# A fused recurrence and mixture-of-experts kernel: the loads of two expert passes are issued later, behind copies of the experts' numbers

## The chip, the cores and the metric

The kernel runs on one core of a Trainium2 chip. A core has five engines that run their own instruction streams: TensorE (PE in the profile; its weight loads are PEld), VectorE (DVE), ScalarE (ACT), GpSimd (POOL) and SyncE (SP). Here SP does little but issue transfers. Transfers run on 16 DMA engines that all queues share. The metric is the device time of one execution in microseconds. Three runs before the change took 410.62, 410.77 and 410.91 us.

## The reference

Two blocks follow each other. The first is a recurrence over 768 steps for 4 batches and 8 heads of dimension 48: a state of 48 x 48 per head decays by a gate, takes in an outer product of key and value, and is read by the query. The second takes the 3072 rows of 384 numbers that come out, chooses one of 4 groups and one of 4 experts in it for every row, and applies that expert's two-layer network.

```python
f = 1.0 / (1.0 + np.exp(-f_logit))
for t in range(S):
    state = f[:, :, t, :, None] * state + np.einsum('bhd,bhe->bhde', k[:, :, t], v[:, :, t])
    y[:, :, t] = np.einsum('bhd,bhde->bhe', q[:, :, t], state)
...
x = attn_out.transpose(0, 2, 1, 3).reshape(B * S, H * D)        # 3072 x 384
g_idx = argmax(x @ w_group)                                     # 4 groups
e_idx = argmax(x @ w_expert[g_idx])                             # 4 experts in each
h = np.maximum(xg[mask_e] @ w1[g, e], 0.0)                      # 384 -> 1024
out[tok_idx] = (g_w * e_w)[:, None] * (h @ w2[g, e])            # 1024 -> 384
```

An expert has 1.57 MB of weights in each of its two layers (w1 and w2); there are 16 experts.

## The kernel before

**Two stages.** Up to about 140 us the recurrence runs in chunks of 128 steps, and each finished chunk is routed: the experts of its rows are chosen and counted, and the rows are written to a table in DRAM (`x_dram`). When the last chunk is routed, the experts have been ranked by their load. `rows_p` then holds, for every place in the ranking, the addresses of the rows of that expert; `who` (cast at L300 in `named`) holds the experts' numbers as integers on one partition.

**Early work.** Places 0 and 1 are fixed before the last chunks: their weights are loaded already during the recurrence (`load_next`, behind copies of their numbers in `who_late`), and `early()` takes 128 rows of each through both layers around 131 to 153 us.

**The passes.** Then come 16 passes, n = 0 to 15, one for each entry of `PLACES`: place 0 again (the rest of its rows), places 2 to 15, and place 1 last. The texts below call n = 1 the second pass and n = 2 the third. A pass has these parts:

- `pass_of(n)` calls `fetch` (L404): indirect gathers of the pass's rows from `x_dram` into a tile `xg`, issued by POOL. Six `xg` tiles exist.
- The rows are turned so that features lie on the partitions, into `xe`: by TensorE with copies behind it (`turn_in`, L440 and L441) for n = 0 and 1 and the last, by VectorE's transposes of 32 x 32 squares (`square_in`, L426) for the others.
- `up` (L450 on TensorE, L451 on ScalarE): the first layer, from `w1`.
- `down` (L486, or `down_rows` at L471 for passes of 128 rows): the second layer, from `w2`.
- The result is turned back (`square_out`, L433), scaled (L458) and scattered to `out` by POOL (L461).

The loop over n is written by hand so that `up` of pass n + 1 stands before `down` of pass n on TensorE. Before the loop, `turn_in(ws[0])`, two steps of `up` of n = 0, `turn_in(ws[1])`, and the rest of `up` of n = 0.

**The loads.** `load_weights` reads one number from `who` into a register of SP (`value`, L388, a TENSOR_LOAD) and issues the transfers of both layers (`load_layer`, L392). The buffers come from two pools: `wp` with two of each layer, which the two early experts hold at first, and `wq` with one of each layer, used by n = 1, 4, 7 and so on. A load waits until the buffer that it takes is no longer read. The engines TensorE, VectorE, ScalarE and SP run in the order in which the code is written (`manual_schedule`); POOL's order is the framework's. So SP issues: both layers of n = 1, both of n = 2, then inside the loop, after each `down(n)`, both layers of n + 3. A waiting load holds up everything behind it on SP.

Of the kernel before, what the change touches and what calls it, by code (L numbers as in the profile page):

```python
# [11 lines left out]
I32 = mybir.dt.int32  # L12
# [11 lines left out]
def kernel(  # L24
# [12 lines left out]
    nc = tc.nc  # L37
# [5 lines left out]
    GE = G * EG  # L43
# [25 lines left out]
    wp = ctx.enter_context(tc.tile_pool(name="wp", bufs=2))  # L69
# [7 lines left out]
    def const(shape, dtype, name):  # L77
        return cp.tile(shape, dtype, tag=name, name=name)

    def bank(shape, name):  # L80
        return ps.tile(shape, FP32, tag="bank", name=name)
# [189 lines left out]
    who = const([1, GE], I32, "who")  # L271
# [115 lines left out]
    def value(ap, top):  # L387
        return nc.values_load(ap, engines=(ET.SP,), min_val=0, max_val=top, skip_runtime_bounds_check_because="a table that the routing makes within these bounds")  # L388

    def load_layer(pool, e, layer):  # L390
        w = pool.tile([P, KO, F] if layer == 1 else [P, FO, DM], FP32, tag=f"w{layer}", name=f"w{layer}")
        nc.sync.dma_start(out=w, in_=(w1v if layer == 1 else w2v)[bass.ds(e, 1)].rearrange("o p k f -> (o p) k f"))  # L392
        return w

    def load_weights(pool, ap):
        e = value(ap, GE - 1)
        return load_layer(pool, e, 1), load_layer(pool, e, 2)
# [9 lines left out]
    def room(w, shape, name):  # L407

        full = w["pool"].tile([P, shape, P if w["pool"] is ep else WIDE], FP32, tag=name, name=name)
        w[name[:2].replace("xe", "xT") + "_full"] = full  # L410
        return full[:, :, 0:w["n"]]

    def squares(w, turn):


        for k_ in range(P // SQ):
            n = sum(j * P + k_ * SQ < w["n"] for j, m in w["blocks"])
            for g in range(P // SQ):
                turn(n, k_, slice(k_ * SQ, (k_ + 1) * SQ), g, slice(g * SQ, (g + 1) * SQ))

    def square_in(w):

        w["xT"] = room(w, KO, "xe")
        x = w["x"][:, :, 0:DM].rearrange("p j (o g c) -> p j g o c", o=KO, c=SQ)
        xT = w["xT_full"].rearrange("p o (j k c) -> p j k o c", j=2, c=SQ)
        squares(w, lambda n, k_, rk, g, rg: nc.vector.transpose(out=xT[rg, 0:n, k_], in_=x[rk, 0:n, g]))  # L426

    def square_out(w):

        w["rows"] = w["pool"].tile([P, 2, DM], FP32, tag="yr", name="yr")  # L430
        y = w["rows"].rearrange("p j (o g c) -> p j g o c", o=KO, c=SQ)
        yT = w["yT_full"].rearrange("p o (j k c) -> p j k o c", j=2, c=SQ)
        squares(w, lambda n, k_, rk, g, rg: nc.vector.transpose(out=y[rk, 0:n, g], in_=yT[rg, 0:n, k_]))  # L433

    def turn_in(w):
        w["xT"] = room(w, KO, "xe")
        for j, m in w["blocks"]:
            pt = bank([P, KO, P], "xg_ps")
            for ko in range(KO):
                nc.tensor.transpose(out=pt[:, ko, 0:m], in_=w["x"][0:m, j, ko * P:(ko + 1) * P], identity=ident[0:m, 0:m])  # L440
            (nc.scalar.copy if w["early"] else nc.vector.tensor_copy)(w["xT"][:, :, j * P:j * P + m], pt[:, :, 0:m])  # L441
# [34 lines left out]
    def down(w, w2):  # L476
        n = w["n"]
        if n == P:
            for _ in down_rows(w, w2):
                pass  # L480
            return
        w["yT"] = w["yT_full"][:, :, 0:n]
        for m in range(KO):
            yp = bank([P, n], "yo")
            for fo in range(FO):
                nc.tensor.matmul(yp, lhsT=w2[:, fo, m * P:(m + 1) * P], rhs=w["h"][:, fo, :], start=(fo == 0), stop=(fo == FO - 1))  # L486
            nc.scalar.copy(w["yT"][:, m, :], yp)  # L487

    def scaled(w, settle=False):
        if w["n"] > P:  # L490
            for j, m in w["blocks"]:
                with settled(settle and j):
                    put(w, j, m, w["rows"][:, j, :])
# [413 lines left out]
    wq = main.enter_context(tc.tile_pool(name="wq", bufs=1))  # L907
# [3 lines left out]
    PLACES = [0] + list(range(EARLY, GE)) + list(range(1, EARLY))  # L911

    def pass_of(n):
        p = PLACES[n]
        if p < EARLY:
            return fetch(mo, rows_p[:, p, 1:2], P)
        return fetch(mo, rows_p[:, p, :], WIDTHS[p - EARLY])

    fari = const([1, 1], I32, "fari")

    def weakest():

        worst = const([P, 1], FP32, "worst")
        nc.vector.tensor_reduce(out=worst, in_=decays.rearrange("p c a n -> p (c a n)"), axis=AX, op=OP.min)
        wt = bank([1, P], "wt")
        nc.tensor.transpose(out=wt, in_=worst, identity=ident)
        far = const([1, 2], FP32, "far")
        nc.vector.tensor_reduce(out=far[:, 0:1], in_=wt, axis=AX, op=OP.min)
        nc.vector.tensor_scalar(far[:, 1:2], far[:, 0:1], math.exp(-SAFE), None, OP.is_lt)
        nc.vector.tensor_copy(fari, far[:, 1:2])  # L930

    def flags():

        nc.vector.tensor_copy(both[:, 0:1], fari)
        nc.vector.tensor_scalar(rest, b_end, 0, None, OP.is_gt)
        nc.vector.tensor_tensor(both[:, 1:2], fari, rest, OP.max)
# [1 line left out]
    both = const([1, 2], I32, "both_i")  # L938
    rest = const([1, 1], I32, "rest")
    ws = {n: pass_of(n) for n in range(3)}  # L940
    ahead = {n: load_weights(wq if n % 3 == 1 else wp, who[0:1, PLACES[n]:PLACES[n] + 1]) for n in range(1, 2)}
    ahead[0] = weights[0]

    def const_out(i):
# [5 lines left out]
    def run_up(n):  # L950
        for _ in up(ws[n], ahead[n][0]):
            pass
# [6 lines left out]
    next(opening)  # L959
    next(opening)  # L960
    turn_in(ws[1])
    for _ in opening:
        pass
    for n in range(GE - 1):
        w = ws[n]
        if n + 3 < GE:
            ws[n + 3] = pass_of(n + 3)
        if n == 0:
            ahead[2] = load_weights(wp, who[0:1, PLACES[2]:PLACES[2] + 1])
        past, coming = ws.pop(n - 1, None), ws.get(n + 2)  # L970
        if past and past["n"] > P:
            square_out(past)
        if coming and coming["n"] > P:
            square_in(coming)
        if n + 2 < GE:
            run_up(n + 1)
        if past:

            scaled(past, n == GE - 3)
        if coming and coming["n"] == P:  # L980
            turn_in(coming)
        w["yT_full"] = outs[n % 2]
        down(w, ahead.pop(n)[1])
        if n + 3 < GE:
            ahead[n + 3] = load_weights(wq if n % 3 == 1 else wp, who[0:1, PLACES[n + 3]:PLACES[n + 3] + 1])
        if n == 2:
            with tc.tile_pool(name="tb", bufs=1) as tb:
                beyond(False, tb)
        if n == 3:
            weakest()  # L990
            flags()
# [133 lines left out]
```

## Time and profile before

| | |
|---|---|
| median of three runs | 410.77 us (410.62 to 410.91) |
| the profiled execution | 410.61 us, of it 408.8 us the span that the profile covers |
| granted TensorE clock, mean | 0.999 |
| TensorE busy | 401.3 us, 98% |
| VectorE busy | 264.9 us, 65% |
| ScalarE busy | 162.9 us, 40% |
| POOL busy | 86.0 us, 21% |
| weight loads on SP's queue | 34 of 1536 KB, 10.9 us median from issue to landing |
| gathers of rows (L404) | 30, 6.7 us median to landing |
| all transfers | 88.99 MB, 218 GB/s over the span |

Times in the profile are microseconds from the start of the span. A row of a group names the line, the engine, the operation, what is written and what is read; a waits row says which engine's line stood idle for whom. Busy times of a pipelined TensorE come with modelled ends.

### The profile page before, as it was taken

The page shows a single profiled execution, that of the slowest core. Times are in us where ns is not written, and L with a number is a line of the kernel's source. Part 1 is how long each engine was busy: PE and PEld are TensorE (multiplying, and loading weights), DVE is VectorE, ACT ScalarE, POOL GpSimd, SP SyncE. Part 2 cuts the span into 40 slices and gives each one's busy share as a digit, 9 for nine tenths or more (in the row PEclk, how much of TensorE's full clock was granted, in tenths as well). Part 3 has the DMA queues.
Part 4 walks back from the last instruction along what each step waited for, and adds up shares of the span by engine and source line. Part 5 has one row for each costly group of instructions (what it writes and reads, how often), then busy time and mean ns, then how long its engine had stood idle before and what let it go on. Part 6 is the DMA issues. An engine that isn't in the chain of part 4 may idle for free.

```text
span 408.8 us, 10274 instructions
## 1 busy us (share of the span) xinstructions
PE 401.3 (98%) x4143; PEld 369.6 (90%) x4143; DVE 264.9 (65%) x783; ACT 162.9 (40%) x365; POOL 86.0 (21%) x132
## 2 busy tenths in 40 slices
PE   8999999999999999999999999999999999999994
PEld 3888888888888969799999999999999999999992
DVE  6666887887998805601999749468576586585230
ACT  6777888888564202121312123122121222222130
POOL 5000010102040084011222123220411310120240
PEclk9999999999999999999999999999999999999999
DMA  9999988789969599993846739468487596485010
GB/s 188 204 216 211 197 176 175 149 164 270 276 214 375 198 319 331 349 326 80 311 138 246 249 135 356 138 257 296 130 327 224 175 354 227 148 314 164 28 50 22
DMA packets 132146, 88.99 MB, mean 218 GB/s; under 512 B 102582, under 2 KB 122748, under 8 KB 132090
## 3 DMA queue, kind: packets, MB, share of 16 engines
q1 hardware_dynamic: 125666, 75.50, 62.0%
q0 software_dynamic: 5792, 11.92, 9.7%
q10 hardware_dynamic: 632, 0.83, 0.6%
q8 instruction: 35, 0.57, 0.5%
q14 instruction: 21, 0.17, 0.1%
HBM read 78.71 MB, written 9.83 MB: 217 GB/s over the span
## 4 chain that ended last, share of the span: by engine, by line
PE 52%; issue 30%; DMA 8%; POOL 6%; DVE 2%; POOLq 1%; ACT 0%; SPq 0%; DVEq 0%
PE hp L450 12%; DMA out_dram<-yt,xg 7%; PE yo L486 7%; PE yo L471 4%; PE cs L616 4%; POOL out_dram L461 4%; PE x_ps L795 3%; PE tr_q L650 3%; PE tr_k L650 3%; PE y L746 3%; PE y L754 2%; PE ap L704 2%; PE ap L689 2%; POOL xg L404 2%; PE ds L722 2%
## 5 line engine op out<-in xcount | busy, mean ns | idle before, releaser
L450 PE MATMUL hp<-xe,w 128*128 128x128 f32 (+14 forms) x864 | 138.6, 320 | 0.0
L450 PEld LDWEIGHTS hp<-xe,w 128*128 128x128 f32 x864 | 135.8, 190 | 0.8
L433 DVE STREAM_TRANSPOSE yr<-yT 32x192 f32<-32x192 f32 (+1 forms) x208 | 70.5, 339 | 70.4 <-ACT yT L487 67.8
L486 PE MATMUL yo<-h,w 128*128 128x230 f32 (+13 forms) x672 | 115.8, 333 | 0.0
L486 PEld LDWEIGHTS yo<-h,w 128*128 128x128 f32 x672 | 113.7, 190 | 0.2
L451 ACT ACTIVATE h<-hp 128x256 f32<-128x256 f32 (+14 forms) x72 | 34.4, 478 | 103.6 <-PE hp L450 103.6
L426 DVE STREAM_TRANSPOSE xe<-xg 32x192 f32<-32x192 f32 (+1 forms) x208 | 69.7, 335 | 8.6 <-PE hp L450 5.6
L461 POOL DMA_INDIRECT out_dram<-yt,xg x32 | 34.5, 1078 | 148.4 <-ACT yt L458 142.8
L487 ACT COPY yT<-yo 128x230 f32<-128x230 f32 (+13 forms) x42 | 13.5, 325 | 80.5 <-PE yo L486 80.5
L404 POOL DMA_INDIRECT xg<-x_dram,rows_p x30 | 29.6, 987 | 53.5 <-DMA out_dram<-yt,xg 29.6
L623 POOL DMA_DIRECT2D ends<-eq x10 | 5.4, 542 | 79.5 <-ACT eq L617 79.5
L471 PE MATMUL yo<-w,h 128*128 128x384 f32 x64 | 21.3, 486 | 0.0
L707 DVE TENSOR_TENSOR am<-ap,tri 128x512 f32<-128x512 f32 x24 | 15.1, 692 | 6.9 <-PE ap L704 6.9
L616 PE MATMUL cs<-ld_f,tri 128*128 128x384 f32 x48 | 18.5, 505 | 0.2 <-ACT ld_f L610 0.2
L471 PEld LDWEIGHTS yo<-w,h 128*128 128x128 f32 x64 | 11.9, 190 | 7.4
L458 ACT ACTIVATE yt<-yr,xg 128x384 f32<-128x384 f32 (+13 forms) x26 | 14.4, 604 | 5.4 <-DVE yr L433 5.4
L757 ACT COPY xT<-y 128x512 f32<-128x512 f32 x24 | 13.4, 587 | 5.5 <-PE y L746 4.4
L650 PE MATMUL tr_q<-ident,qh 128*128 128x128 f32 x96 | 14.5, 273 | 0.5 <-issue 0.5
L651 ACT COPY Tk<-tr_k 128x512 f32<-128x512 f32 x24 | 14.8, 621 | 0.0
L651 ACT COPY Tq<-tr_q 128x512 f32<-128x512 f32 x24 | 14.6, 607 | 0.4 <-PE tr_q L650 0.3
L692 DVE TENSOR_TENSOR am<-ap,seen 128x384 f32<-128x384 f32 x24 | 12.2, 552 | 3.8 <-PE ap L689 3.8
L650 PE MATMUL tr_k<-ident,kh 128*128 128x128 f32 x96 | 14.3, 273 | 0.0
(187 smaller groups left out, 433.8 us busy)
## 6 DMA issues: line engine op xcount, KB each, us to landing
w<-in_moe_w_dram SPq DMA_DIRECT2D x34, 1536.0 KB, 10.9
qh<-in_q_dram SPq DMA_DIRECT2D x12, 384.0 KB, 5.0
ld_k<-in_k_dram SPq DMA_DIRECT2D x12, 384.0 KB, 5.5
v<-in_v_dram SPq DMA_DIRECT2D x12, 384.0 KB, 5.7
ld_f<-in_f_logit_dram SPq DMA_DIRECT2D x11, 384.0 KB, 5.3
x_dram<-x_kept SPq DMA_DIRECT2D x2, 1536.0 KB, 8.3
x_dram<-x POOLq DMA_DIRECT2D x2, 384.0 KB, 4.3
x_dram<-x ACTq DMA_DIRECT2D x2, 384.0 KB
```

The source lines that it names most:

```text
L404: nc.gpsimd.indirect_dma_start(out=w["x"][:, j, :], out_offset=None, in_=x_dram[0:1 + top, :], in_offset=bass.IndirectOffsetOnAxis(ap=rows ...
L426: squares(w, lambda n, k_, rk, g, rg: nc.vector.transpose(out=xT[rg, 0:n, k_], in_=x[rk, 0:n, g]))
L433: squares(w, lambda n, k_, rk, g, rg: nc.vector.transpose(out=y[rk, 0:n, g], in_=yT[rg, 0:n, k_]))
L450: nc.tensor.matmul(hp[:, o, :], lhsT=w1[:, ko, (f + o) * P:(f + o + 1) * P], rhs=w["xT"][:, ko, :], start=(ko == 0), stop=(ko == KO - 1))
L451: nc.scalar.activation(h[:, f:f + 2, :], hp, AF.Relu)
L461: sent = nc.gpsimd.indirect_dma_start(out=out, out_offset=bass.IndirectOffsetOnAxis(ap=w["x"][0:m, j, DM + 1:RW].bitcast(U32), axis=0), in ...
L471: nc.tensor.matmul(yp, lhsT=w["h"][:, fo, :], rhs=w2[:, fo, :], start=(fo == 0), stop=(fo == FO - 1))
L486: nc.tensor.matmul(yp, lhsT=w2[:, fo, m * P:(m + 1) * P], rhs=w["h"][:, fo, :], start=(fo == 0), stop=(fo == FO - 1))
L616: nc.tensor.matmul(cs.rearrange("t h d -> t (h d)"), lhsT=tri, rhs=nl[:, b], start=True, stop=True)
L650: nc.tensor.transpose(out=pt[:, a, :], in_=w[nm + "h"][:, b, 2 * a:2 * a + 2, :].rearrange("t r d -> t (r d)"), identity=ident)
L651: nc.scalar.copy(w["T" + nm][:, b], pt)
L707: nc.vector.tensor_tensor(am[:, r], ap[r], tri.unsqueeze(1).broadcast_to((P, HP, P)), OP.mult)
```

## The change

The loads of n = 1 and n = 2 are taken apart. Only the first layer of n = 1 is still loaded at the old place. A new function, `next_name(n)`, has VectorE copy one number from `who` to a tile `who_next`; SP's register is then loaded from that tile, so SP waits for VectorE to reach that copy. Both layers of n = 2 are issued behind such a copy after `turn_in(ws[1])`. The second layer of n = 1 is issued behind another one at n = 0 of the loop, after `square_in` of n = 2. The order on SP becomes: n = 1 first layer; n = 2 both layers; n = 1 second layer; n = 3 both layers; and on as before. The order of POOL's instructions, of ScalarE's and of TensorE's stays.

```diff
     fari = const([1, 1], I32, "fari")
+    who_next = const([1, GE], I32, "who_next")
+
+    def next_name(n):
+
+        p = PLACES[n]
+        nc.vector.tensor_copy(who_next[:, p:p + 1], who[:, p:p + 1])
+        return value(who_next[0:1, p:p + 1], GE - 1)
+
...
-    ahead = {n: load_weights(wq if n % 3 == 1 else wp, who[0:1, PLACES[n]:PLACES[n] + 1]) for n in range(1, 2)}
+    first_name = value(who[0:1, PLACES[1]:PLACES[1] + 1], GE - 1)
+    ahead = {1: [load_layer(wq, first_name, 1)]}
     ahead[0] = weights[0]
...
     turn_in(ws[1])
+    e = next_name(2)
+    ahead[2] = load_layer(wp, e, 1), load_layer(wp, e, 2)
     for _ in opening:
         pass
     for n in range(GE - 1):
         w = ws[n]
         if n + 3 < GE:
             ws[n + 3] = pass_of(n + 3)
-        if n == 0:
-            ahead[2] = load_weights(wp, who[0:1, PLACES[2]:PLACES[2] + 1])
         past, coming = ws.pop(n - 1, None), ws.get(n + 2)
         if past and past["n"] > P:
             square_out(past)
         if coming and coming["n"] > P:
             square_in(coming)
+        if n == 0:
+            ahead[1].append(load_layer(wq, next_name(1), 2))
         if n + 2 < GE:
             run_up(n + 1)
```

## The prediction

> **What bounds the kernel now.** I read the slices of the page first, then who waited for whom, then the chain in order of time, and only then the queues. The slices, PE and DMA, 10.2 us each:
>
> ```profile
> PE   8999999999999999999999999999999999999994
> DMA  9999988789969599993846739468487596485010
> ```
>
> TensorE (PE) is over 90% busy in every slice but the first and the last; DMA has holes. The waits of PE, all that the profile has of them:
>
> ```profile
> PE warm L893 <- DVE onesb L107: 1.1, 1, 1.1
> PE tr_q L650 <- issue: 0.5, 1, 0.5
> PE cs L616 <- ACT ld_f L610: 0.2, 1, 0.2
> ```
>
> Columns are total, times, longest in us. None names the expert stage (L440 to L513), and none names a weight load. The chain in order of time around the change:
>
> ```profile
> 153.16 2.68 PE hp L450 x24
> 155.83 0.59 PE xg_ps L440 x6
> 156.43 12.02 PE hp L450 x72
> 168.45 5.16 PE yo L471 x16
> 173.61 9.00 PE hp L450 x48
> 182.61 9.32 PE yo L486 x48
> 191.93 8.68 PE hp L450 x48
> 200.61 9.00 PE yo L486 x48
> ```
>
> Each piece begins where the one before ends. I call the passes n = 0, 1, 2, 3 (n = 1 is the "second pass"). The 72 are 24 matmuls of n = 0 and 48 of the first layer of n = 1: 24 at the 111.7 ns of the first row (2.68 us / 24) are 2.68 us, which leaves 9.34 us, so n = 1 begins at 159.1. The other side of a check: 48 matmuls of the same 230 columns take 9.32 us in the row at 182.61. So nothing waits there either. The deadlines read off: first layer of n = 2 at 173.6 (its weight load into PE starts at 173.13), second layer of n = 1 at 182.3 (first weight load at 182.26), first layer of n = 3 at 191.6, second of n = 2 at 200.3. Two results: nothing in these 50 us can be shortened by an earlier arrival, since PE waits for none; and the change costs just what a load comes later than its deadline.
>
> **The change part by part.** Timeline rows (start, duration, what), then the groups of the name loads and the landings of all weight loads (min/median/max, in ns for the first row, in us for the second):
>
> ```profile
> 153.19 0.37 SPq L392 DMA_DIRECT2D w<-in_moe_w_dram  x1
> 156.68 0.47 DVE L441 COPY xe<-xg_ps 128x306 f32<-128x306 f32 x1
> 159.16 6.67 SPq L392 DMA_DIRECT2D w<-in_moe_w_dram  x1
> 159.17 5.71 DVE L426 STREAM_TRANSPOSE xe<-xg 32x192 f32<-32x192 f32 x16 [2.02 <-PE hp L450]
> 168.49 5.71 DVE L426 STREAM_TRANSPOSE xe<-xg 32x192 f32<-32x192 f32 x16 [3.61 <-PE hp L450]
> ```
>
> ```profile
> L388 SPq TENSOR_LOAD <-who x15: 264/268/281, 142.2 to 355.8; - x15
> DMA to landing us min/median/max: 6.9/10.9/13.9
> ```
>
> Before, SyncE (SP) issues: n = 1 first layer at 143.09, n = 1 second at 143.66, n = 2 first at 144.62, n = 2 second at 153.19 (behind early work that frees its buffer), n = 3 first at 159.16, n = 3 second at 173.64. After, its order is: n=1 first | wait for copy A | n=2 first, n=2 second | wait for copy B | n=1 second, n=3 first, n=3 second.
>
> *Copies on VectorE.* Two of one element; the nearest row is another 1x1 integer cast of this kernel (b_end, L368): 0.14 us. Copy A follows the L441 copy that ends at 157.15, and VectorE then stands until 159.17 for PE: its cover is that 2.02 us. Copy B follows the 16 transposes that end at 164.88, with 3.61 us of idle behind. Cost 0; uncovered it would be 0.3 us of VectorE, which still ends the transposes of n = 2 at 165.2, before 173.1.
>
> *Name loads on SP.* One more TENSOR_LOAD, 0.27 us. From the end of the cast of the names (142.14) to the issue at 143.09 took 0.95 us, all of load, register operations and issue; a second load with the same name came 0.57 us later, one with a new name 0.96 us later.
>
> *n = 2, both layers, behind copy A.* 157.15 + 0.14 + 0.95 = 158.25 for the first, 158.8 for the second; before, 144.6 and 153.2. Both buffers are free by then (the second's since the row at 153.19). Landing: the median 10.9 gives 169.2, the longest of the run 13.9 gives 172.2; the deadline is 173.1. In time by 3.9 us, at the worst by 0.9. The second is wanted at 200.3, over 40 us later.
>
> *n = 1 second layer behind copy B.* 164.88 + 0.14 + 0.95 = 166.0, 22.3 us later than before. Median 176.9, longest 179.9, deadline 182.26: in time by 5.4, at the worst 2.4.
>
> *n = 3, queued behind that wait on SP.* First layer at 166.0 + 0.96 = 166.95 in place of 159.16; longest landing 180.9, and if SP is held at the issue as long as it was at 159.16 (6.67 us), 187.5; deadline 191.6. Its second layer waits for n = 0 to end at 173.6 as before; a hold of 6.67 us from 166.95 ends at 173.6 too, so nothing moves there. The load of n = 4 (174.5) keeps its place.
>
> *The same sums by bytes.* Windows (PE, PEld, DVE, ACT, POOL busy, clock, DMA share, GB/s):
>
> ```profile
> 165.00:167.00 2.00, 2.00 (x12) 1.96 (x11) 0.00 (x0) 0.55 (x1) 0.00 (x0) 1.00 1.03 397
> 171.00:173.00 2.00, 2.00 (x8) 1.20 (x7) 1.93 (x6) 0.00 (x0) 0.00 (x0) 1.00 0.62 247
> 173.00:175.00 2.00, 2.00 (x11) 1.74 (x10) 1.15 (x5) 0.58 (x1) 0.50 (x1) 1.00 0.56 188
> 187.00:189.00 2.00, 2.00 (x12) 1.96 (x11) 0.00 (x0) 0.14 (x1) 0.00 (x0) 1.00 0.05 19
> ```
>
> A load is 1536 KB, 1.57 MB. At some 370 GB/s it is 4.25 us. Before, DMA moves 63 GB/s from 143 to 145 (2 us to start), over 290 in every 2 us to 171, then has the hole of the two middle rows to about 176, and is done at 187. After, from 158.25 on there are four loads and two scatters of 0.2 MB: with 2 us to start, n=2 first is in at 165, n=2 second at 169, n=1 second at 174, n=3 first at 178, and the two loads issued at 173.6 and 174.5 at about 187. The hole takes up the work that was put off; no later stage sees it.
>
> *POOL and the gathers.* POOL's order does not change. Its 11 gathers of x (143.0 to 157.2, 6.5 to 10.0 us to land) meet one weight load instead of three and land earlier. What is gained by it: PE takes up the transposes of n = 0 and n = 1 without a wait at 150.4 and 155.6, VectorE those of n = 2 at 159.17 for PE's sake; so 0. A loss is excluded, a gain bounded by the 0.18 us of gap in front of one PE weight load at 150.7.
>
> **Two rules of the Trainium skill weighed.** The table "Rules for kernel authors" in "DMA: Bandwidth & Descriptors" says to issue a DMA early and wait on its semaphore late; the change does the reverse for three loads, so the rule would have it slower. The row: landings of 6.9 to 13.9 us against 14.9 us (n = 2) and 16.3 us (n = 1) left between the new issue and the deadline. By the row the sum is +0; the rule would give something only from a landing over 14.9 us on. The same page's section "Queues, rings and completion order" says that completion is not first in, first out, and that speaks against my sums by bytes. The trace has two loads issued 0.87 us apart, at 173.64 and 174.51:
>
> ```profile
> DMA to landing us min/median/max: 9.4/10.9/12.3
> ```
>
> The first took 9.4, the second 12.3: in at 183.0 and 186.8, 3.8 us apart, about one load's 4.25; in order, not side by side. If they did share evenly: at 166.0, 0.85 MB of n=2 second are left, and three loads at a third of 370 GB/s finish that at 172.9; then the two left have 0.7 MB each, joined at 173.6 by two more, done four abreast near 180.5, and with the way to the semaphore 181.5. Still 0.8 us before 182.26. By the rule +0 as well, with a thin margin; I take the row.
>
> **Sum.** 0 + 0 + 0 + 0 on a profiled execution of 410.61 us (span 408.8, and 1.81 around it). The median of the runs is 410.77, 0.16 above it. Forecast for the median: 410.8.
>
> **The rivals.**
> *A, slower: the second layer of n = 1 comes late.* Place: PE at 182.3, down of n = 1. SP may be held at that issue as it was at 159.16 (6.67 us), because two loads are still under way: then 166.0 + 6.67 + 10.9 = 183.6, a stall of 1.3 us, 412.1; with the longest landing 4.3 us, 415.1. It decides from 16.3 us between issue and landing. For it: a load issued while others ran did hold SP twice (2.92 and 6.67). Against: at 166.0 the first load of n = 2 is in or nearly so by bytes, and bytes, not the hold, set the landing. A stall here is not given back, PE having no idle.
> *B, slower at n = 2:* the same at 173.1, from 14.9 us on; at 16 us it costs 1.1, 411.9. Against: only part of the late gathers and two scatters lie in front of it.
> *C, faster: gathers on a freer DMA let the expert stage begin earlier.* For it: gathers take up to 10.0 us under three loads. Against: PE waits for none of them; at most 0.18, 410.6. For a gain of 0.8 us the stage before would have to end earlier, and nothing of it is touched.
> *D, the change does nothing,* since the loads are hidden either way: 410.8, the forecast itself.
> *E, PE slowed by DMA traffic that moved:* excluded, 48 matmuls of 230 columns took 9.34 us from 159.1 on, at 329 to 403 GB/s, and 9.32 us from 182.6 on, at 8 to 292 GB/s.
>
> **How the numbers follow.** No change (with D): 0.79. A: 0.11, B: 0.05. C or something unseen that helps: 0.05. Within 0.2% means within 0.82 us, about what a measurement of this kernel can tell from no change. Same 0.79, slower 0.16, faster 0.05. The range runs from 410.2 (C with the spread of runs, 410.62 to 410.91, twice over) to 412.1, the plain case of A, which leaves out A's worst end. The likeliest case alone: 410.5 to 411.1.
>
> **What would show it.** Right: SP waits for VectorE twice, loads issued near 158.3, 158.8, 166.0 and 167.0; no PE wait behind a weight load; chain pieces at 173.6, 182.6 and 191.9 as now, within 0.3 us; the DMA hole moved from 172 to 176 to before 158. Wrong: a gap in PE at 182.3 (A) or 173.1 (B), with landings over 14.9 us; or n = 0 beginning before 153.0 (C). The forecast fails if landings behind two loads are much longer than any here, or if PE's ends as modelled hide a wait that the gathers caused.

## The result and the profile after

The changed kernel takes 412.4 us (median of 15 runs, 411.79 to 413.89) against 410.77 us (15 runs, 410.55 to 411.13). The ratio is 1.0041, interval 1.0035 to 1.0048: slower by about 1.6 us. The forecast was 410.8 us, no change, with a range up to 412.1: the kernel became slower, and the time lies 0.3 us above that range. The profiled execution took 412.37 us with a span of 410.5.

First the part the prediction was about. Timeline of the changed kernel around the two copies (start, duration, what):

```profile
158.64 0.13 DVE L925 COPY who_next<-who 1x1 int32<-1x1 int32 x1
159.32 1.00 SPq L392 DMA_DIRECT2D w<-in_moe_w_dram  x2
160.75 5.71 DVE L426 STREAM_TRANSPOSE xe<-xg 32x192 f32<-32x192 f32 x16 [1.98 <-PE hp L450]
166.49 0.14 DVE L925 COPY who_next<-who 1x1 int32<-1x1 int32 x1
167.14 1.74 SPq L392 DMA_DIRECT2D w<-in_moe_w_dram  x2
```

Everything here is 1.6 us later than in the time frame of before. Taken off, the copies stand at 157.05 and 164.90 and the loads go out at 157.7, 158.3, 165.6 and 166.4, all within 0.6 us of what was forecast. And the chain in order of time:

```profile
154.75 2.68 PE hp L450 x24
157.42 0.59 PE xg_ps L440 x6
158.01 12.02 PE hp L450 x72
170.04 5.16 PE yo L471 x16
175.20 9.00 PE hp L450 x48
184.20 9.32 PE yo L486 x48
193.52 8.68 PE hp L450 x48
202.20 9.00 PE yo L486 x48
```

The durations are those of before and each piece begins where the last ended. No load is late, and of the waits of TensorE none is in the expert stage (L440 to L513):

```profile
PE warm L893 <- DVE onesb L107: 1.1, 1, 1.1
PE tr_q L650 <- DVE qh L636: 0.5, 1, 0.5
PE y L754 <- issue: 0.2, 1, 0.2
PE rk L213 <- DVE ohe L208: 0.2, 1, 0.2
```

But the chain's first line is at 154.75, where before it was at 153.16: the time was lost before the changed loads are even issued. The same landmarks of the chain, before and after, tell where (start in us):

| landmark on TensorE | before | after | later by |
|---|---|---|---|
| 4 matmuls of L616, third row of L616 in the chain before | 22.75 | 23.73 | 0.98 |
| 4 matmuls of L616, sixth row of L616 in the chain before | 49.88 | 51.35 | 1.47 |
| L213 (rank of a chunk) | 100.90 | 102.48 | 1.58 |
| first layer of the early experts, 36 matmuls | 132.83 | 134.41 | 1.58 |
| first steps of pass n = 0 | 153.16 | 154.75 | 1.59 |
| second layer of n = 1 | 182.61 | 184.20 | 1.59 |

The recurrence stage, whose code the change does not touch, is slower by all of it. The row for SP's queue before, then the slices of DMA and the same row after (the slices of before stand in the prediction; the row has packets, MB, and the share of the 16 engines' span that the packets took):

```profile
q1 hardware_dynamic: 125666, 75.50, 62.0%
```

```profile
DMA  9999999999999776993847649478496596485010
q1 hardware_dynamic: 125666, 75.50, 68.1%
```

The same packets and the same bytes need 0.681 x 16 x 410.5 = 4473 us of engine time in place of 0.620 x 16 x 408.8 = 4055. The slices place the excess: where before had 8s and a 7 from 51 to 92 us and a 6 at 112, the changed kernel has 9s up to 133. From 10 to 40 us (columns: PE, PEld, DVE, ACT, POOL busy; clock; DMA share; GB/s), before and after:

```profile
10.00:40.00 30.00, 30.00 (x550) 25.48 (x550) 20.31 (x51) 22.75 (x47) 1.57 (x3) 1.00 1.04 210
```

```profile
10.00:40.00 30.00, 29.91 (x550) 25.18 (x549) 19.62 (x48) 22.48 (x46) 1.57 (x3) 1.00 1.25 184
```

More busy time for fewer bytes. The DMA issues of the page, in KB each and us to landing, before and after:

```profile
qh<-in_q_dram SPq DMA_DIRECT2D x12, 384.0 KB, 5.0
ld_k<-in_k_dram SPq DMA_DIRECT2D x12, 384.0 KB, 5.5
v<-in_v_dram SPq DMA_DIRECT2D x12, 384.0 KB, 5.7
ld_f<-in_f_logit_dram SPq DMA_DIRECT2D x11, 384.0 KB, 5.3
```

```profile
qh<-in_q_dram SPq DMA_DIRECT2D x12, 384.0 KB, 7.2
ld_k<-in_k_dram SPq DMA_DIRECT2D x12, 384.0 KB, 6.4
v<-in_v_dram SPq DMA_DIRECT2D x12, 384.0 KB, 7.1
ld_f<-in_f_logit_dram SPq DMA_DIRECT2D x11, 384.0 KB, 6.4
```

The landings of q and v grow most. How this reaches TensorE shows in the chain after, which now runs through SP's queue and a load of k, and in the waits up to 62 us:

```profile
8.68 1.75 SPq L591
...
10.47 7.62 DMA ld_k<-in_k_dram
...
18.19 0.56 DVE kh L639
...
20.43 0.66 PE tr_k L650 x4
```

```profile
DVE kh L639 <- DMA ld_k<-in_k_dram: 1.8, 2, 1.6
DVE qh L636 <- DMA qh<-in_q_dram: 1.2, 1, 1.2
```

Before, the first of these two waits has 0.6 us and the second does not exist. VectorE's products `kh` and `qh` come late, and with them TensorE's transposes of k: the first of them, at 9.65 in place of 9.00, by 0.65 us, and from those at 20.43 on everything by the 0.98 us of the table's first row. The next 0.49 us fall inside the matmuls of L754, which took 1.63 us in one piece before (from 45.39) and 2.12 us after:

```profile
46.37 0.69 PE y L754 x19
47.06 0.24 issue
47.30 1.19 PE y L754 x45
```

Here the profile names no releaser ("issue"), so that this part too comes from the slower transfers is not shown by the trace. The experiments below bear on it.

What can the change have done to loads that come 100 us before it? One part of it had not been costed: `who_next = const([1, GE], I32, ...)` is a new tile of 64 bytes per partition in the first pool. The addresses of the two built programs show that all pools behind it move by 64 bytes. A load of q or v writes rows of 48 numbers, 192 bytes, into a tile with 256 bytes per row. Before, that tile began at byte 32 of a 256-byte block (address 162336), and a row covered bytes 32 to 224. After, it begins at byte 96 (162400), and every row runs from 96 to 288, over the end of the block. ld_f and ld_k are packed at 192 bytes per row; half of their rows cross such a boundary at either place.

### The profile page after: what moved, and what is told of

Same layout as the page of the kernel before. It is cut to its first block, busy times and chain, and to the rows that moved or that the text cites. A ratio compares the mean times of both kernels' runs of the same rounds, so it can differ in the third digit from the quotient of the medians.

```text
span 410.5 us, 10277 instructions
## 1 busy us (share of the span) xinstructions
PE 402.6 (98%) x4143; PEld 370.3 (90%) x4143; DVE 265.4 (65%) x785; ACT 163.4 (40%) x365; POOL 84.3 (21%) x132
## 3 DMA queue, kind: packets, MB, share of 16 engines
q1 hardware_dynamic: 125666, 75.50, 68.1%
## 4 chain that ended last, share of the span: by engine, by line
PE 49%; issue 30%; DMA 9%; POOL 6%; DVE 3%; SPq 2%; POOLq 1%; DVEq 0%
PE hp L450 12%; DMA out_dram<-yt,xg 7%; PE yo L486 7%; PE yo L471 4%; POOL out_dram L461 4%; PE cs L616 3%; PE x_ps L795 3%; PE y L754 2%; SPq L591 2%; PE tr_k L650 2%; PE ap L689 2%; POOL xg L404 2%; PE tr_q L650 2%; PE y L746 2%; PE y L742 2%
## 5 line engine op out<-in xcount | busy, mean ns | idle before, releaser
L450 PE MATMUL hp<-xe,w 128*128 128x128 f32 (+14 forms) x864 | 138.6, 320 | 0.0
L450 PEld LDWEIGHTS hp<-xe,w 128*128 128x128 f32 x864 | 135.8, 191 | 0.8
L616 PE MATMUL cs<-ld_f,tri 128*128 128x384 f32 x48 | 19.0, 522 | 0.0
```

The lines of the kernel that those rows point to most:

```text
L450: nc.tensor.matmul(hp[:, o, :], lhsT=w1[:, ko, (f + o) * P:(f + o + 1) * P], rhs=w["xT"][:, ko, :], start=(ko == 0), stop=(ko == KO - 1))
L616: nc.tensor.matmul(cs.rearrange("t h d -> t (h d)"), lhsT=tri, rhs=nl[:, b], start=True, stop=True)
```

## The experiments

The theories were L, that the place of these pieces in SBUF costs the time, and O, that the new order or the copies do. The experiments ran on three chips: e1 to e4 and e11 to e13 on one, e5 to e8 on a second, e9 and e10 on a third. On each of them the kernel before takes some 5 us more than in the first comparison (medians of 416.0 to 416.4 us), so times are compared only as ratios to the kernel before on the same chip. There is no trace of the kernel before from these chips; in the traces of e1, e2, e4 and e9 TensorE pauses around 160 us, and the granted clock falls to 0.5 behind it in the first three. Why it pauses is not known. The share of SP's queue in the profiles is the finer measure: multiplied by 16 and the span it gives the engine time of the same 125666 packets.

**e1: the tile alone.** The kernel before, with a tile of that size that nothing uses.

```diff
     fari = const([1, 1], I32, "fari")
+    const([1, 16], I32, "spare")
```

> The kernel before with one unused tile of 64 bytes per partition where the changed kernel has who_next; order of loads as before. Theory L (the tile shifts all later pools by 64 bytes, so that the 192-byte pieces of q and v, which started at byte 32 of a 256-byte block, start at byte 96 and cross its end): as slow as the changed kernel, 412.4 us, and SP's queue takes about 68% of the 16 engines' span in place of 62%. Theory O (the new order of the weight loads or the copies on VectorE cost the time): 410.8, 62%.

Measured: 418.87 against 416.2 us, ratio 1.0068 (1.0051 to 1.0085).

```profile
q1 hardware_dynamic: 125666, 75.50, 67.0%
```

An unused tile makes the kernel slower, with every load where it was.

**e2: the change without the shift.** The changed kernel, its tile four times as wide.

```diff
-    who_next = const([1, GE], I32, "who_next")
+    who_next = const([1, 4 * GE], I32, "who_next")
```

> The changed kernel with who_next widened from 64 to 256 bytes, so that the later pools shift by 256 bytes and keep their place within a 256-byte block; order of loads as in the changed kernel. Theory L: 410.8 us, 62% of the span in SP's queue. Theory O: 412.4, 68%.

Measured: 416.25 against 416.2 us, ratio 1.0001 (0.9986 to 1.0016).

```profile
q1 hardware_dynamic: 125666, 75.50, 61.0%
```

The new order of loads with both copies costs nothing that can be measured. Theory O falls; e1 and e2 together carry L.

**e3 and e4: which tiles.** Spare bytes in the pools inside the first stage.

```diff
# e3: 64 bytes ahead of q, v and the other padded tiles
+        kept([P, 16], "spare")
         pads = {}
```

> The kernel before with 64 unused bytes at the head of the pool that holds q, v and the padded work tiles; ld_f, ld_k and the weights stay where they were. Theory L, if the pieces of q and v are what matters: 412.4 us, SP's queue at 68%. If the shift of ld_f, ld_k or of the weight buffers matters instead: 410.8, 62%.

```diff
# e4: 64 bytes ahead of ld_f and ld_k, 192 more ahead of q and v
+        sb.tile([P, 16], FP32, tag="spare_sb", bufs=1, name="spare_sb")
         later = sums.tile([P, 2, HP, D], FP32, tag="ds", name="ds")
...
+        kept([P, 48], "spare")
         pads = {}
```

> The reverse: ld_f and ld_k shifted by 64 bytes, q and v by 256 (no change within a block), weights not at all. Of the pieces of ld_f and ld_k, which are packed at 192 bytes, half cross a 256-byte block at either start. Theory L with q and v: 410.8 us, 62%. If ld_f and ld_k matter: up to 412.4.

Measured: e3 419.92 us, ratio 1.0087 (1.0057 to 1.0117); e4 416.05 us, 0.9993 (0.998 to 1.0006). The queue's row of e3, then of e4:

```profile
q1 hardware_dynamic: 125666, 75.50, 66.7%
```

```profile
q1 hardware_dynamic: 125666, 75.50, 60.9%
```

It is the pool that holds q and v, the two tensors of that pool that transfers write. The same shift of ld_f and ld_k is free. A rival is that the work tiles in that pool, which compute engines read and write, are slower at the new place; but the products that read them take the same time (L636 on 128 x 768 numbers: 953 ns before, after and in e1), and it is the engine time of transfers that grew.

**e5 to e8: how the cost goes with the start.** The changed kernel again, and the kernel before with an unused tile of 32, 128 and 224 bytes in the place of e1's.

> The changed kernel as it is, beside the three that follow on one chip. Its pieces of q and v start at byte 96 of a 256-byte block and all cross its end; half of those of ld_f and ld_k do. Three quarters of all pieces cross, against one quarter before. Both theories below: about 1.004 to 1.007 times the time before, SP's queue at 67 to 68%.

> The kernel before with 32 unused bytes: q and v start at byte 64 and end with the block, none crosses; of ld_f and ld_k three quarters cross in place of half. Theory X (each piece that crosses a 256-byte block costs a fixed extra): 3/8 of all pieces cross against 1/4 before and 3/4 after, a quarter of the loss: 63 to 64% in SP's queue, 1.001 to 1.002 in time. Theory B (a piece costs the 32-byte steps from the block's start to its end, as the skill's page on DMA counts an access that starts inside a block): q and v 8 steps, ld_f and ld_k 10 on the mean, together 9, just as the changed kernel's 9 and 9: 68%, 1.004 to 1.007.

> 128 unused bytes: q and v start at byte 160, all cross a 256-byte block, and of ld_f and ld_k half. Theory X: as the changed kernel, 67 to 68%, 1.004 to 1.007. Theory B: q and v 11 steps, ld_f and ld_k 9, together 10 against 8 before and 9 after: 73 to 74%, over 1.01. A theory of 128-byte lines (three touched at byte 96, two at bytes 32 and 160): as before, 62%.

> 224 unused bytes: q and v start at byte 0, none crosses; of ld_f and ld_k three quarters cross. Theory X: 3/8 of all, as with 32 bytes, 63 to 64%, 1.001 to 1.002. Theory B: 6 and 10 steps, together 8, as before: 62%, 1.000.

The page meant in e6 (theory B) is "DMA: Bandwidth & Descriptors" of the Trainium skill, section "How a descriptor splits into AXI transactions". It says that a transaction may read less than 256 bytes but starts at an address aligned to 256, so that a descriptor that starts inside such a block has a first transaction that begins at the block's start, and what lies before the data still costs 32-byte beats.

| kernel | q and v start at byte | rows that cross: q, v / ld_f, ld_k | ratio to before (interval) | SP's queue |
|---|---|---|---|---|
| e5, the change | 96 | all / half | 1.0083 (1.0059 to 1.0108) | 66.6% of 416.5 |
| e6, 32 bytes | 64 | none / three quarters | 1.0011 (0.9998 to 1.0025) | 62.0% of 415.2 |
| e7, 128 bytes | 160 | all / half | 1.0079 (1.0058 to 1.01) | 66.3% of 418.6 |
| e8, 224 bytes | 0 | none / three quarters | 1.0009 (0.9998 to 1.002) | 62.1% of 414.8 |

Theories X and B are far apart in e6 and e7, and both runs go against beats: e6 would have had 68% and e7 over 73. A theory of 128-byte lines falls with e7. What the four agree with is a step: a row of q or v pays when it crosses the end of a block, and how far into the block it starts makes no difference. That is what the page's count of transactions (one or two) would say, where its count of beats does not. The page words it for reads and these rows are written into SBUF; no run here shows the transactions themselves.

e6 and e8 are not quite free. Their engine time is 4119 and 4121 us, some 70 above e4's 4051, where theory X with its 63 to 64% put somewhat more. No row of q and v crosses in them, but a quarter more of the rows of ld_f and ld_k does. Put down to those 12288 rows it is some 6 ns each, an estimate; the weight buffers moved too, and no run parts the two.

**e9: no row crosses.** ld_f and ld_k at 256 bytes per row, on block starts, with q and v kept at byte 32.

```diff
-                    w[nm] = sb.tile([P, 2, H, D], FP32, tag="ld_" + nm, bufs=3 if nm == "f" else 2, name="ld_" + nm)
+                    w[nm] = sb.tile([P, 2, H, DP], FP32, tag="ld_" + nm, bufs=3 if nm == "f" else 2, name="ld_" + nm)[:, :, :, 0:D]
...
-            nl = w["f"].rearrange("p b h d -> p b (h d)")
+            nl = w["f"]
...
-                nc.tensor.matmul(cs.rearrange("t h d -> t (h d)"), lhsT=tri, rhs=nl[:, b], start=True, stop=True)
+                nc.tensor.matmul(cs, lhsT=tri, rhs=nl[:, b], start=True, stop=True)
```

> The kernel before (its order of loads) with ld_f and ld_k held at 256 bytes a row in place of 192, starting on a block, and with spare bytes that keep q and v at byte 32: of all pieces none crosses a 256-byte block. Theory X: a quarter of all pieces less crosses than before, so half of the loss of the changed kernel's DMA share is won on the other side: SP's queue at some 58 to 59% where the kernel before has 61 on this chip; the time 0.998 to 1.000, as TensorE has little idle in the first stage to give back. If packing at 192 bytes costs nothing by itself: 61%, 1.000.

Measured: 416.17 against 416.35 us, ratio 1.0004 (0.9991 to 1.0016).

```profile
q1 hardware_dynamic: 125666, 75.50, 61.1%
```

A miss: nothing is won. The half of ld_f and ld_k that crosses in the packed tiles was costing nothing, or the wider rows cost as much as was gained by having no crossings. It also was the candidate for a kernel better than both, and is not.

**e10: a load that is really late.** The layout of e2, but the second layer of n = 1 one turn of the loop later.

```diff
-        if n == 0:
+        if n == 1:
             ahead[1].append(load_layer(wq, next_name(1), 2))
```

> The changed kernel with who_next widened to 256 bytes (the layout of before), and copy B with the second layer of the second pass one turn of the loop later still, behind the transposes of pass n = 3 and behind both layers of n = 3 on SP. It puts the deadline reckoning of the prediction to the test. By it: issue near 175, 9.4 to 12.3 us to land as for two loads in a row, so 184 to 187 against the 182.3 at which TensorE needs it: a gap there of 2 to 5 us, and 1.005 to 1.012 in time, all of it kept to the end. If TensorE's deadlines are not what decides: 1.000.

Measured: 420.09 against 416.35 us, ratio 1.0075 (1.0049 to 1.01). Its wait of TensorE, and its chain:

```profile
PE yo L486 <- DMA w<-in_moe_w_dram: 2.8, 1, 2.8
```

```profile
181.04 10.40 DMA w<-in_moe_w_dram
191.44 0.14 issue
191.58 11.01 PE yo L486 x48
```

Issued at 181.04, landed 10.40 us later, and TensorE stood for 2.8 us: this is how a load behind its deadline looks. With that chip's pause all of it stands some 6 us later than expected, but the reckoning foresaw the size of the gap. The loss is larger than the gap: the 48 matmuls behind it took 11.01 us, against 9.32 in the changed kernel, and the granted clock from 192 to 194 us was 0.50. The changed kernel has no such row.

**e11 to e13: what sort of crossing costs.** e11 is e9 with the spare tile of ld_f and ld_k widened from 64 to 160 bytes, so that their rows, now apart, all cross (q and v stay put). e12 and e13 are e3 with 160 and 96 spare bytes.

```diff
# e11, against e9
-        sb.tile([P, 16], FP32, tag="spare_sb", bufs=1, name="spare_sb")
+        sb.tile([P, 40], FP32, tag="spare_sb", bufs=1, name="spare_sb")
...
-        kept([P, 48], "spare")
+        kept([P, 24], "spare")
```

> As the run with ld_f and ld_k at 256 bytes a row, but these two start at byte 96 of a block, so that all of their pieces cross its end; q and v stay at byte 32, none crosses. Theory X1 (a piece that stands apart from its neighbours costs extra when it crosses a block, whatever tensor it is; pieces packed without gaps cost little): half of all pieces pay, as in the changed kernel: 66 to 67% in SP's queue, 1.006 to 1.008. If there is something particular to q and v: 61%, 1.000.

> The kernel before with 160 unused bytes at the head of the pool of q and v alone: they start at byte 192, all cross a block, but their start is a multiple of 64 bytes (64 bytes before the boundary, 128 behind). Theory X1: 66 to 67%, 1.006 to 1.008. Theory X2 (a crossing costs only where the start is no multiple of 64 bytes, as at 96 and 160): 61%, 1.000; it would explain why the half of ld_f and ld_k that cross, at 128 and 192, cost nothing.

> The same with 96 unused bytes: q and v start at byte 128, all cross, a multiple of 128 bytes (128 before the boundary, 64 behind). Theory X1: 66 to 67%. Theory X2: 61%.

Measured: e11 1.003 (1.0014 to 1.0045), e12 1.0052 (1.0025 to 1.0078), e13 1.0061 (1.0046 to 1.0077). The queue's rows, in this order:

```profile
q1 hardware_dynamic: 125666, 75.50, 64.3%
```

```profile
q1 hardware_dynamic: 125666, 75.50, 67.3%
```

```profile
q1 hardware_dynamic: 125666, 75.50, 67.0%
```

e12 and e13 cross at starts that are multiples of 64 bytes and pay in full, so X2 falls. e11 shows that the loss is not tied to q and v: rows of ld_f and ld_k pay too once they stand apart and cross. They pay about half, though, where X1 foresaw the whole. In engine time (share x 16 x span):

| which rows cross | kernels | us |
|---|---|---|
| of the packed rows half, or (e9) no row at all | before in the first comparison, e2, e4, e9, e10 | 4038 to 4066 |
| of the packed rows three quarters | e6, e8 | 4119, 4121 |
| all of ld_f and ld_k, held apart | e11 | 4286 |
| all of q and v | the change twice, e1, e3, e7, e12, e13 | 4438 to 4500 |

The 24 loads of q and v are 49152 rows. Against e4's 4051, a crossing row costs (4477 - 4051) us / 49152 = 8.7 ns in q and v (e1), and e11 against e9 gives (4286 - 4038) / 49152 = 5.0 ns in ld_f and ld_k. Why the two differ stays open. So does what a packed row costs that crosses: nothing by e9 against e4, some 6 ns by e6 and e8. e9 took away the packing and the crossing at once, and no run parts them.

That the time goes in the first stage on these chips too is read ahead of the pause. The early experts' first layer (the row of 36 matmuls of L450) begins at 132.7 to 133.7 us in the traces of the table's first two rows, at 134.0 in e11, and at 134.4 to 136.4 in all seven with q and v crossing. The wait in L754 fits this: it is listed, with 0.2 to 0.4 us, in six of those seven traces, and with 0.2 in one of the eight others.

## Why the prediction was wrong

**The part on the loads was right in what it said of the deadlines.** Copies in VectorE's idle time: 0.13 and 0.14 us, as forecast. From a copy's end to the issue: 0.55 and 0.51 us, where the forecast took 0.95 from the cast of the names. The deadlines held with no TensorE wait, and the two loads behind n = 0 landed 9.4 and 12.8 us after issue (9.4 and 12.3 before), and DMA was done by about 188; shifted back by 1.6 that is 186.4, where the forecast had 187. The hole in DMA moved to the time before the loads of n = 2: 153, 149 and 184 GB/s in the three windows from 153 to 159. Both rules of the Trainium skill weighed in the prediction, on early issue and on completion order, made no difference, as the rows said. e2 puts the worth of the whole reordering at 1.0001, and e10 shows that the deadline reckoning would have caught a real miss. One term of it does not follow from its own sums: the check with even sharing starts from 0.85 MB left of n = 2's second layer at 166.0, where the sum by bytes (in at 169, 370 GB/s) leaves 1.1 MB. With 1.1 the load would still be in time, by some 0.4 us in place of 0.8 (an estimate from the prediction's own numbers).

**The step that failed** is in the list of parts and in the sum "0 + 0 + 0 + 0". The forecast went through copies, name loads, transfers and gathers; it left out the tile that the copies write, and so put the stage ahead of them at nothing. Rival C closed the matter with "nothing of it is touched", said of that stage. That held for its instructions and not for the addresses that they write. The runs put in place of the 0: some 420 us of engine time in the first stage's transfers, and 1.58 us of TensorE before the expert stage begins (e1 is slower by 1.0068 with that tile alone, e2 is rid of the loss with 192 bytes more). For 1.0 us of the 1.58 the trace shows the way, through SP's issues and VectorE's first products; for 0.5 us in L754 it names no releaser. Of the prediction's signs of being right the pieces of the chain "as now, within 0.3 us" failed, by 1.6 us; of its signs of being wrong none came, because none was set for a first stage that ends later.

**Rivals A and B** gave the right sign with the wrong mechanism. 412.1 for A is close to 412.4 by accident; by the total alone A would have seemed right. The chain's start at 154.75 refutes it in one line.

**The spread** of the changed kernel's runs, 2.1 us against 0.6 before, was not foreseen either. It goes with a first stage in which DMA is over 90% busy in every slice; that this is its cause was not tried.

## What to carry to other kernels

A new tile is part of a change even if it is small: compare the addresses of the tiles that later pools hold, above all of those that many small pieces are loaded into, before costing anything at zero. When the profile of a changed kernel is shifted, line up the same landmark of the chain in both traces from the front, and look for the first one that differs; it can lie far ahead of the edited lines. And separate "the edit's order" from "the edit's allocation" with two runs: the old order with the new tile, and the new order with the old addresses.

## What the runs showed of the hardware that was not expected

192-byte rows of q and v, written by transfers from DRAM into SBUF with 256 bytes between row starts, cost 8 to 9 ns more of a DMA engine's time each if they cross a 256-byte boundary of the partition's address, whether they start at byte 96 (the change, e1, e3), 128 (e13), 160 (e7) or 192 (e12). At 32 (before, e2, e4) they do not; at 0 and 64 (e8, e6) the whole queue took 70 us more than in e4, a sixth of that loss, with other rows crossing. Rows of ld_f and ld_k at the same spacing cost 5 ns more each when they cross (e11). For a kernel whose first stage keeps DMA busy, the crossing of q and v was 0.4% of the time in the first comparison, and 0.5 to 0.9% on the chips of the experiments. How much of the difference between the chips is the transfers' share was not tried.
